# Lightning attention and MLP on one core: pair 5 in chunks of 64 tokens, pair 7 in two parts, v loads behind transposes

## The chip, the core and the metric

The kernel runs on one core of a Trainium2 chip. The metric is the device time in microseconds (us) of one execution; the profile of one execution gives the span from its first to its last instruction and what every engine did in it. The engines are PE (matrix products, results in PSUM), DVE (vector), ACT (scalar activations), POOL (GpSimd) and SP, whose queue issues nearly all DMAs of this kernel in the order in which they stand in it.

## The reference

Inputs q, k, v have the shape (batch 4, heads 8, tokens 768, dim 64). First comes a causal attention with a decay per head, block by block of 64 tokens with a running 64x64 state; then a residual MLP with normalisation. Cut to what matters:

```python
for b in range(nb):                       # nb = 768 / 64
    intra = einsum('bhic,bhjc->bhij', qb, kb) * Dmask        # Dmask: lam^(i-j), causal
    intra = einsum('bhij,bhjd->bhid', intra, vb)
    inter = einsum('bhid,bhde->bhie', qb * lam_pow, kv_state)
    out[:, :, sl] = intra + inter
    kv_state = lam_block * kv_state + einsum('bhsd,bhse->bhde', kb * rev_pow, vb)
x = out.transpose(0, 2, 1, 3).reshape(4, 768, 512)
xn = (x - mean(x)) / sqrt(var(x) + 1e-6) * g_ln
y = x + maximum(xn @ w_ch1, 0) @ w_ch2     # w_ch1 512x2048, w_ch2 2048x512
```

The answer doesn't depend on the block length: with the matching powers of the decay a block may have 128 tokens as well.

## The kernel before

A work unit, called a pair below, is one batch element's 256 tokens: two tiles of 128. There are 12 of them, u = 0 to 11; u % 4 is the batch element, u // 4 the third of the sequence. Each pair goes through the same steps:

- `load_one` or `load_window`: k, q, v from HBM to SBUF (tags kin, qin, vin, three buffers each). Pairs below `LB` are loaded by one DMA of 512 KB for each tensor with runs of 512 bytes (L71), two neighbouring tokens in a row; the others by two DMAs of 256 KB with runs of 256 bytes (L75), one token in a row.
- `p0`: POOL casts k (`in_k`, L199), scales q and casts it (`in_q`, L210) and scales v into vb (`in_v`, L216).
- `transpose_dma`: two DMA transposes on SP make kqT from kq (L231); pairs 0 to 2 use PE instead (L224).
- For a pair below `LB`, in chunks of 128: `kv` (L281, 32 matmuls of 64x64, out to pk), `scores` in two halves (L247, 16 matmuls each with 128 columns), `mask` on DVE (L257, four of 128x512), `new_state` (DVE add L291, POOL decay L287), `av` (L393, 64 matmuls of 64x64), `inter` twice (L406, 16 matmuls each).
- For the others, in chunks of 64: `kv64` (L346, 32), `scores64` (L327, 32 with 64 columns), `mask64` (L333, two of 128x512), `states64` twice (two DVE adds L362 and L365, POOL decay L287 and a cast L370), `av64` (L380, 32), `inter` twice. `keep64` is their mask, made by `make_keep64`.
- `norm`: ACT copies po to x (L428), DVE takes statistics (L430, L431) and writes xc (L435). `to_xT`: a DMA transpose on SP for each tile makes x^T (L451).
- The MLP of the pair (`mlp`): 8 items m1 of 8 matmuls with 128x256 (L484), each followed by ACT's relu (L487), then 8 items m2 of 4 matmuls with 128x512 (L522), four for each tile, after which DVE adds x (`finish`, L543) and SP stores the rows (L550).

Nothing is ordered by a scheduler: `manual_schedule` keeps the order in which the program calls the steps. Pairs 0 and 1 are written out by hand; there L484 stands between their attention steps by `m1s(m1a, chunk, lo, hi)`, which runs a part of the MLP items of pair 0 that use one of the four chunks of w1. All else hangs on one list, `plan`, of MLP items in the order in which PE runs them: n = 0 to 5 finish pair 1's m1, 6 to 21 are m2 of pairs 0 and 1, and from 22 on 16 items belong to each pair from 2 on (pair 3 from 38, pair 4 from 54, pair 5 from 70). `add(n, (step, ...))` puts steps behind item n: each engine and queue gets its instructions at that place of its own order. Pair 6 has its pieces merged with those of pair 5 in two parts, `X1` at n = 56 and `X2` at n = 60; from pair 7 on all is one part, `X`, at n = 73, 89 and so on.

Every DMA of SP signals on one of eight semaphores in turn, and a DMA waits until the one eight places before it has landed. PSUM has four buffers of tag mm, which the MLP's pm and the attention's pk share, two of tag sc and one each of po0 and po1.

Of the kernel before, what the change touches and what calls it, by code (L numbers as in the profile page):

```python
# [16 lines left out]
def kernel(  # L17
# [11 lines left out]
    nc = tc.nc  # L29
# [7 lines left out]
    NP = H // 2  # L37
# [15 lines left out]

    half = [slice(0, 64), slice(64, 128)]
    XB = 3
    LB = 6

    def mm_tile(shape, dtype, name):
        return ps.tile(shape, dtype, tag="mm", bufs=4, name=name)
# [8 lines left out]
    def fill(got, name, u, hs):  # L68
        src = dict(k=k, q=q, v=v)[name]
        if u < LB:  # L70
            nc.sync.dma_start(got[:, hs], source(src, u, hs))  # L71
# [6 lines left out]
    def load_one(u, name):  # L78
        got = inp.tile([128, H, 2 * D], F32, tag=name + "in", name=name + "in")
        fill(got, name, u, slice(0, H))  # L80
        qkv_in.setdefault(u, {})[name] = got.rearrange("p h (j d) -> p h j d", j=2)

    def load_window(u, after_pool=False, parts=1):
        got = {name: inp.tile([128, H, 2 * D], F32, tag=name + "in", name=name + "in") for name in "kqv"}
        if after_pool:

            nc.gpsimd.memset(got["k"][:, 0, 0:1], 0.0)
        n = H // parts
        order = [(name, i) for i in range(parts) for name in "kq"] + [("v", i) for i in range(parts)]
        for name, i in order:  # L90
            hs = slice(i * n, (i + 1) * n)
            fill(got[name], name, u, hs)
        qkv_in[u] = {name: f.rearrange("p h (j d) -> p h j d", j=2) for name, f in got.items()}
# [107 lines left out]
    def in_q(u, eng, hs=ALL):  # L201
        src = qkv_in[u]["q"][:, hs].rearrange("p (a e) j d -> p a e j d", e=2)
        dst = part(1, st[u]["kq"], hs)
        if u < LB:
            lq = lam_q[:, hs, :].rearrange("p (a e) j -> p a e j", e=2)
# [7 lines left out]
    def in_v(u, eng, hs=ALL):  # L213
        n = hs.stop - hs.start
        lv = lam_v[:, hs, :, None] if u < LB else lam_p[:, 1, hs, None, None]
        eng.tensor_tensor(st[u]["vb"][:, hs], qkv_in[u]["v"][:, hs], lv.to_broadcast([128, n, 2, D]), op=ALU.mult)  # L216
# [53 lines left out]
    def kv(u, tag="mm"):  # L270

        s = st[u]
        cc, b = divmod(u, B)
        n_ab = 2 if (cc + 1) * W < S else 1
        bufs = dict(mm=4, sc=2, po=1)[tag]
        pk = [ps.tile([128, 2, NP, D], F32, tag=f"po{ab}" if tag == "po" else tag, bufs=bufs, name=f"pk{ab}")[:, 0] for ab in range(n_ab)]
        for p in range(NP):
            for j in range(2):
                for e in range(2):
                    for ab in range(n_ab):  # L280
                        nc.tensor.matmul(pk[ab][half[e], p, :], lhsT=s["kq"][half[ab], 0, p, j, e],  # L281
                                         rhs=s["vb"][half[ab], 2 * p + e, j],
                                         start=(p == 0 and j == 0), stop=(p == NP - 1 and j == 1), skip_group_check=True)
        s["pk"] = pk
# [46 lines left out]
    def mask64(u, e):  # L331
        s = st[u]
        nc.vector.tensor_tensor(s["mA"][:, e], s["sc"][e],  # L333
                                keep64[:, None, None, :].to_broadcast([128, NP, 2, D]), op=ALU.mult)
# [38 lines left out]
    def av64(u):  # L373
        s = st[u]
        s["po"] = [ps.tile([128, H, D], F32, tag=f"po{ab}", name=f"po{ab}") for ab in range(2)]
        for p in range(NP):
            for e in range(2):
                for j in range(2):
                    for ab in range(2):
                        nc.tensor.matmul(s["po"][ab][half[j], 2 * p + e, :], lhsT=s["mA"][half[ab], e, p, j],  # L380
                                         rhs=s["vb"][half[ab], 2 * p + e, j],
                                         start=(p == 0 and e == 0), stop=False, skip_group_check=True)

    def av(u, pairs, chunks=(0, 1)):
        s = st[u]
        if "po" not in s:
            s["po"] = [ps.tile([128, H, D], F32, tag=f"po{ab}", name=f"po{ab}") for ab in range(2)]
        for p in pairs:
            for e in range(2):
                for j in range(2):  # L390
                    for jq in range(2):
                        for ab in chunks:
                            nc.tensor.matmul(s["po"][ab][half[jq], 2 * p + e, :],  # L393
                                             lhsT=s[f"mA{p // 2}"][half[ab], e, p % 2, j, half[jq]],
                                             rhs=s["vb"][half[ab], 2 * p + e, j],
                                             start=(p == 0 and e == 0 and j == 0), stop=False, skip_group_check=True)
# [22 lines left out]
    def norm(u, ab, early=False):  # L419
        s = st[u]  # L420
        po = s["po"][ab].rearrange("p h d -> p (h d)")
        if "x" not in s:
            s["x"] = xp.tile([128, 2, DM], F32, tag="x", name="x")
            s["mv"] = xp.tile([128, 2, 2], F32, tag="mv", name="mv")
            s["xc"] = wk.tile([128, 2, DM], BF16, tag="xc", name="xc")
        x, mv, xc = s["x"][:, ab], s["mv"][:, ab], s["xc"][:, ab]
        if not early:
            nc.scalar.copy(x, po)  # L428
        stats = wk.tile([128, 6], F32, tag="stats", name="stats")
        nc.vector.bn_stats(stats, po if early else x)  # L430
        nc.vector.bn_aggr(mv, stats)  # L431
        n_h = 2 if u == 0 else 1
        for h in range(n_h):
            sl = slice(h * DM // n_h, (h + 1) * DM // n_h)
            nc.vector.scalar_tensor_tensor(xc[:, sl], in0=po[:, sl], scalar=mv[:, 0:1], in1=g_row[:, sl],  # L435
                                           op0=ALU.subtract, op1=ALU.mult)
# [92 lines left out]
    def rows_of(u):  # L529

        cc, b = divmod(u, B)
        order = "(c p j) d -> j p c d" if u < LB else "(j c p) d -> j p c d"
        return out[b, cc * W:(cc + 1) * W, :].rearrange(order, c=2, j=2)
# [104 lines left out]
    m1a, m2a = mlp(0)  # L638
    m1b, m2b = mlp(1)

    def m1s(f, c, lo=0, hi=2):
        n = f.count // NWC
        for u in range(c * n + lo * n // 2, c * n + hi * n // 2):
            f(u)
# [17 lines left out]
    mask(1, 0)  # L662
    mask(1, 1)
    m1s(m1a, 1, 0, 1)
    kv(1, "sc")
    new_state(1, 0, nc.scalar)
    m1s(m1a, 1, 1, 2)
    rstd_of(0)
    m1s(m1a, 2, 0, 1)
    av(1, (0, 1))  # L670
# [21 lines left out]
    load_w2(3)  # L692
    in_v(2, nc.gpsimd)
    load_window(3, after_pool=True)
    load_window(4)

    def p0(u, k_eng=None):
        open_window(u)
        in_k(u, k_eng or nc.gpsimd)
        in_q(u, nc.gpsimd)  # L700
        in_v(u, nc.gpsimd)

    def s0(u):
        kv(u, "po")
# [15 lines left out]
    def wind_up(u):  # L720


        s = st[u]
        if u < LB:
            av(u, range(NP))
# [71 lines left out]


    def X1(u):
        av(u - 1, range(NP))  # L800
        inter(u - 1, 0)
        kv64(u)
        states64(u, 0)
        states64(u, 1)

    def X2(u):
        scores64(u)
        inter(u - 1, 1)
        mask64(u, 0)
        norm(u - 1, 0)  # L810
        norm(u - 1, 1)
        mask64(u, 1)

    def X(u):

        if u - 1 < LB:
            av(u - 1, range(NP))
# [25 lines left out]
    def add(at, *steps):  # L843
        after.setdefault(at, []).extend(steps)
# [6 lines left out]
    add(8, (s0, 2))  # L851
    add(10, (s3, 2))
    add(12, (s4, 2), (p4, 2), (p0, 3, nc.vector), (transpose_dma, 3))
    for n, name in zip((14, 15, 16), "kqv"):
        add(n, (load_one, 5, name))
    add(15, (rstd_of, 2))
    add(17, (p0, 4))
    add(25, (s1, 3))
    add(25, (transpose_dma, 4))
    add(27, (s2, 3))  # L860
    add(28, (p0, 5))
    add(29, (s3, 3))
    add(30, (s4, 3), (p4, 3))
    for n, name in zip((30, 31, 32), "kqv"):
        add(n, (load_one, 6, name))
    add(34, (rstd_of, 3), (make_keep64,))
    add(37, (transpose_dma, 5))
    add(38, (s1, 4))
    add(39, (p0, 6))
    add(40, (s2, 4))  # L870
    add(42, (s3, 4))
    add(44, (s4, 4), (p4, 4))
    add(46, (transpose_dma, 6))
    add(50, (s1, 5), (rstd_of, 4))
    add(53, (s2, 5))
    for j in range(6, NU):
        at = 55 + 16 * (j - 6)
        if j > 6:
            for n, name in zip((23, 21, 19), "kqv"):
                add(at - n, (load_one, j, name))  # L880
            add(at - 13, (p0, j))
            add(at - 8, (transpose_dma, j))
        if j < LB:
            add(at, (s1_s3, j))
            add(at + 4, (s2_s4, j), (p4, j - 1))
        else:
            if j == 6:
                add(at + 1, (X1, j))
                add(at + 5, (X2, j), (p4, j - 1))
            else:  # L890
                add(at + 2, (X, j), (p4, j - 1))
        add(at + 9, (rstd_of, j - 1))
# [34 lines left out]
```

## Time and profile before

| | |
|---|---|
| median of 10 runs | 216.37 us (214.58 to 218.42) |
| the profiled execution | 217.85 us, its span 216.1 us |
| PE busy, matmuls | 202.8 us (94%), 2884 |
| DVE, ACT, POOL busy | 103.3, 87.3, 79.8 us |
| mean granted PE clock | 0.991 |
| L484 (m1), L522 (m2) | 87.9 us and 81.1 us busy |
| DMA | 37.13 MB, 68385 of 94142 packets under 512 bytes |

Between the span and the execution's time lie 1.75 us of start and end. In a line of the timeline the columns are the start in us from the span's start, the length in us, the engine (PEld is PE's weight load, SPq the DMAs that SP issues), the line of the kernel, the operation, out<-in, the shapes and how many instructions were merged; the bracket is the idle time of the engine before it and what ended it. In a line of the stretches the columns are the stretch, its length, the busy time and the count of PE, PEld, DVE, ACT and POOL, the granted clock of PE, the share of the DMA engines and GB/s.

### The profile page before, as it was taken

The page shows a single profiled execution, that of the slowest core. Times are in us where ns is not written, and L with a number is a line of the kernel's source. Part 1 is how long each engine was busy: PE and PEld are TensorE (multiplying, and loading weights), DVE is VectorE, ACT ScalarE, POOL GpSimd, SP SyncE. Part 2 cuts the span into 40 slices and gives each one's busy share as a digit, 9 for nine tenths or more (in the row PEclk, how much of TensorE's full clock was granted, in tenths as well). Part 3 has the DMA queues.
Part 4 walks back from the last instruction along what each step waited for, and adds up shares of the span by engine and source line. Part 5 has one row for each costly group of instructions (what it writes and reads, how often), then busy time and mean ns, then how long its engine had stood idle before and what let it go on. Part 6 is the DMA issues. An engine that isn't in the chain of part 4 may idle for free.

```text
span 216.1 us, 6642 instructions
## 1 busy us (share of the span) xinstructions
PE 202.8 (94%) x2884; PEld 138.3 (64%) x2899; DVE 103.3 (48%) x225; ACT 87.3 (40%) x165; POOL 79.8 (37%) x111
## 2 busy tenths in 40 slices
PE   2988799999999999999999999999999999999992
PEld 0466579644685575585586585684784874865862
DVE  2688263448256445746438256165184292532011
ACT  3766548511253145055064163271370460641610
POOL 4745339147546073219118229047065020000000
PEclk9999799999999999999999999999999999999999
DMA  4999999999899899699799999998999611320304
GB/s 118 292 272 208 214 255 163 226 298 229 188 317 176 188 211 185 95 221 213 129 217 205 139 227 192 176 201 185 206 210 169 149 25 30 99 52 0 97 2 96
DMA packets 94142, 37.13 MB, mean 172 GB/s; under 512 B 68385, under 2 KB 91169, under 8 KB 94114
## 3 DMA queue, kind: packets, MB, share of 16 engines
q1 hardware_dynamic: 89584, 32.38, 72.3%
q0 software_dynamic: 4224, 4.19, 12.3%
q8 instruction: 22, 0.36, 0.7%
q10 hardware_dynamic: 306, 0.14, 0.3%
q14 instruction: 6, 0.05, 0.1%
HBM read 27.27 MB, written 6.29 MB: 155 GB/s over the span
## 4 chain that ended last, share of the span: by engine, by line
PE 85%; DMA 6%; SPq 3%; DVE 2%; issue 1%; POOL 1%
PE pm L484 37%; PE pm L522 37%; DMA vin<-in_v_dram 6%; SPq L71 3%; PE pm2h L513 2%; PE po L393 1%; PE po L406 1%; PE sc L247 1%; PE po L380 1%; PE pk L281 1%; POOL vb L216 1%; PE sc L327 1%; PE pm1t L496 1%; PE pk L346 1%; DVE xc L435 1%
## 5 line engine op out<-in xcount | busy, mean ns | idle before, releaser
L487 ACT ACTIVATE hT<-pm 128x512 bf16<-128x512 f32 x92 | 55.0, 601 | 90.9 <-PE pm L484 90.8
L484 PE MATMUL pm<-xT,w 128*128 128x256 bf16 x736 | 87.9, 276 | 1.0 <-DMA w<-in_moe_w_ch_dram 0.8
L522 PE MATMUL pm<-w,hT 128*128 128x512 bf16 x353 | 81.1, 379 | 1.0 <-issue 0.3
L484 PEld LDWEIGHTS <-w 128*128 128x128 bf16 x736 | 70.7, 99 | 13.4 <-DMA w<-in_moe_w_ch_dram 1.0
L522 PEld LDWEIGHTS <-hT 128*128 128x128 bf16 x368 | 35.5, 98 | 40.0
L543 DVE SCALAR_TENSOR_TENSOR o<-pm,rstd,x 128x512 f32<-128x512 f32 x23 | 17.1, 748 | 43.4 <-PE pm L522 43.3
L287 POOL TENSOR_TENSOR Sn<-Stmp,lam_s 128x256 bf16<-128x256 f32 x16 | 9.8, 614 | 73.7 <-DVE Stmp L365 49.6
L435 DVE SCALAR_TENSOR_TENSOR xc<-po,mv,g_row 128x512 bf16<-128x512 f32 (+1 forms) x24 | 16.8, 705 | 1.8
L257 DVE TENSOR_TENSOR mA<-sc,keep 128x512 bf16<-128x512 f32 x20 | 13.1, 684 | 6.8 <-PE sc L247 6.8
L428 ACT COPY x<-po 128x512 f32<-128x512 f32 x18 | 9.9, 588 | 11.3 <-PE po L393 5.3
L430 DVE BATCH_NORM_STATS2 stats<-x 128x6 f32<-128x512 f32 x18 | 12.4, 687 | 4.0 <-ACT x L428 3.9
L417 DVE COPY seen<-po 128x8 f32<-128x8 f32 x18 | 2.3, 162 | 23.8 <-PE po L406 23.8
L216 POOL TENSOR_TENSOR vb<-vin,lam_v 128x1024 bf16<-128x1024 f32 (+1 forms) x7 | 11.6, 1658 | 4.4 <-DMA vin<-in_v_dram 3.4
L210 POOL TENSOR_TENSOR kq<-qin,lam_p 128x512 bf16<-128x512 f32 x12 | 12.3, 1044 | 0.7 <-DMA qin<-in_q_dram 0.7
L210 POOL TENSOR_TENSOR kq<-qin,lam_q 128x512 bf16<-128x512 f32 x10 | 10.6, 1084 | 3.8 <-DMA qin<-in_q_dram 3.8
L216 POOL TENSOR_TENSOR vb<-vin,lam_p 128x1024 bf16<-128x1024 f32 x6 | 11.4, 1898 | 1.0 <-DMA vin<-in_v_dram 0.9
L199 POOL CAST kq<-kin 128x512 bf16<-128x512 f32 (+1 forms) x18 | 10.5, 613 | 1.6 <-DMA kin<-in_k_dram 1.6
L333 DVE TENSOR_TENSOR mA<-sc,keep 128x512 bf16<-128x512 f32 x12 | 8.2, 682 | 1.4 <-PE sc L327 1.4
L406 PE MATMUL po<-Sn,kqT 64*64 64x64 bf16 x216 | 7.5, 199 | 0.0
L224 PE MATMUL tp<-ident,kq 128*128 128x128 bf16 x48 | 6.0, 262 | 0.5 <-ACT kq L199 0.2
L406 PEld LDWEIGHTS <-kqT 64*64 64x64 bf16 x304 | 5.3, 108 | 1.5 <-issue 1.5
L224 PEld LDWEIGHTS <-kq 128*128 128x128 bf16 x48 | 3.7, 112 | 3.9 <-DVE kq L199 1.5
(98 smaller groups left out, 145.9 us busy)
## 6 DMA issues: line engine op xcount, KB each, us to landing
out_dram<-o SPq DMA_DIRECT2D x22, 256.0 KB, 4.6
w<-in_moe_w_ch_dram POOLq DMA_DIRECT2D x8, 512.0 KB, 9.2
kin<-in_k_dram SPq DMA_DIRECT2D x14, 256.0 KB, 3.6
qin<-in_q_dram SPq DMA_DIRECT2D x14, 256.0 KB, 5.0
vin<-in_v_dram SPq DMA_DIRECT2D x14, 256.0 KB, 5.9
kin<-in_k_dram SPq DMA_DIRECT2D x5, 512.0 KB, 6.2
qin<-in_q_dram SPq DMA_DIRECT2D x5, 512.0 KB, 7.6
vin<-in_v_dram SPq DMA_DIRECT2D x5, 512.0 KB, 8.4
```

Of the source, the lines that this page charges most:

```text
L199: (eng.copy if eng is nc.scalar else eng.tensor_copy)(dst[:, :, :, j], src[:, :, :, j])
L210: eng.tensor_tensor(dst[:, :, :, j], src[:, :, :, j], lq[:, :, :, j:j + 1].to_broadcast([128, n, 2, D]), op=ALU.mult)
L216: eng.tensor_tensor(st[u]["vb"][:, hs], qkv_in[u]["v"][:, hs], lv.to_broadcast([128, n, 2, D]), op=ALU.mult)
L257: nc.vector.tensor_tensor(s[f"mA{hf}"][:, e], s[f"sc{hf}"][e], kp[:, None, :, :].to_broadcast([128, 2, 2, 128]), op=ALU.mult)
L406: nc.tensor.matmul(s["po"][ab][half[jq], 2 * p + e, :], lhsT=qT[half[e], p, jq, half[ab]], rhs=s["S"][ab][jq][half[e], p, :], start=False, ...
L428: nc.scalar.copy(x, po)
L430: nc.vector.bn_stats(stats, po if early else x)
L435: nc.vector.scalar_tensor_tensor(xc[:, sl], in0=po[:, sl], scalar=mv[:, 0:1], in1=g_row[:, sl], op0=ALU.subtract, op1=ALU.mult)
L484: nc.tensor.matmul(pm[:, b, :], lhsT=w1[n // W2K][:, kk, (n % W2K) * 128:(n % W2K + 1) * 128], rhs=xT_of[g][:, kk, 0:N], start=(b == 0 and ...
L487: nc.scalar.activation(hT[:, u * NB:(u + 1) * NB, 0:N], pm, ACT.Relu)
L522: nc.tensor.matmul(acc[i], lhsT=hT[:, kk, i * 128:(i + 1) * 128], rhs=w2[kk // W2K][:, kk % W2K, :], start=(kk == 0), stop=(kk == KB - 1))
L543: nc.vector.scalar_tensor_tensor(o[:, ab], in0=a, scalar=rstd[:, ab:ab + 1], in1=x[:, ab], op0=ALU.mult, op1=ALU.add)
```

## The change

Pair 5 is now in the group with chunks of 64 (`LB` 6 to 5): a new step `A(5)` at n = 51 does its kv64, scores64, masks and states in one piece, and `X1` and `X2` use `av64`. Pair 7 also goes by `X1` and `X2`, at n = 72 and 76. In the hand-written part a stretch of pair 0's MLP stands ahead of pair 1's `kv` rather than behind it. The v loads of pairs 4, 5 and 6 are issued later on SP, each behind the x^T transposes of an earlier pair (2, 3 and 4), and `in_v` of these pairs is taken out of `p0` and stands later on POOL. The steps of pair 4 stand two or three items later, and its k/q transposes behind the x^T transposes of pair 3.

```diff
-    LB = 6
+    LB = 5
...
     m1s(m1a, 1, 0, 1)
+    m1s(m1a, 1, 1, 2)
     kv(1, "sc")
     new_state(1, 0, nc.scalar)
-    m1s(m1a, 1, 1, 2)
...
-    load_window(4)
+    load_one(4, "k")
+    load_one(4, "q")
...
     def p0(u, k_eng=None):
...
-        in_v(u, nc.gpsimd)
+        if u not in (4, 5, 6):
+            in_v(u, nc.gpsimd)
...
     def X1(u):
-        av(u - 1, range(NP))
+        av64(u - 1)
...
+    def A(u):
+        kv64(u)
+        scores64(u)
+        states64(u, 0)
+        mask64(u, 0)
+        states64(u, 1)
+        mask64(u, 1)
...
-    for n, name in zip((14, 15, 16), "kqv"):
+    for n, name in zip((18, 19, 31), "kqv"):
         add(n, (load_one, 5, name))
-    add(17, (p0, 4))
+    add(17, (load_one, 4, "v"), (p0, 4))
     add(25, (s1, 3))
-    add(25, (transpose_dma, 4))
     add(27, (s2, 3))
-    add(28, (p0, 5))
+    add(31, (p0, 5))
     add(29, (s3, 3))
-    add(30, (s4, 3), (p4, 3))
-    for n, name in zip((30, 31, 32), "kqv"):
+    add(30, (s4, 3), (p4, 3), (transpose_dma, 4))
+    for n, name in zip((32, 33), "kq"):
         add(n, (load_one, 6, name))
+    for n, u in ((26, 4), (43, 5), (52, 6)):
+        add(n, (in_v, u, nc.gpsimd))
     add(37, (transpose_dma, 5))
-    add(38, (s1, 4))
-    add(39, (p0, 6))
-    add(40, (s2, 4))
-    add(42, (s3, 4))
-    add(44, (s4, 4), (p4, 4))
-    add(46, (transpose_dma, 6))
-    add(50, (s1, 5), (rstd_of, 4))
-    add(53, (s2, 5))
+    add(41, (s1, 4))
+    add(42, (p0, 6))
+    add(43, (s2, 4))
+    add(44, (s3, 4))
+    add(46, (s4, 4), (p4, 4))
+    add(46, (load_one, 6, "v"), (transpose_dma, 6))
+    add(51, (A, 5), (rstd_of, 4))
...
-            if j == 6:
+            if j in (6, 7):
                 add(at + 1, (X1, j))
                 add(at + 5, (X2, j), (p4, j - 1))
```

## The prediction

> **What bounds the kernel now.** I read the page's busy rows first, then its slices, then the stretches of the matrix engine's clock, then the timeline around the two places that the diff touches.
>
> ```profile
> PE 202.8 (94%) x2884; PEld 138.3 (64%) x2899; DVE 103.3 (48%) x225; ACT 87.3 (40%) x165; POOL 79.8 (37%) x111
> PE   2988799999999999999999999999999999999992
> PEclk9999799999999999999999999999999999999999
> ```
>
> PE is busy all the time but in slices 0 to 4 (5.4 us each), so after 27 us only PE work removed or a new PE wait can move the end. The one dip of the clock is in slice 4. Busy time by stretches of 3.41 us around it:
>
> ```profile
> 20.99:24.41 3.42, 1.48 (x41) 1.19 (x42) 1.84 (x4) 1.70 (x3) 2.12 (x3) 1.00 1.24 206
> 24.41:27.82 3.41, 3.41 (x19) 2.18 (x16) 0.17 (x1) 1.71 (x6) 0.00 (x0) 0.50 1.14 243
> ```
>
> The first column after the stretch's length is PE busy, the third from the end the granted clock. PE is busy for 1.48 of 3.42 us, and in the next stretch it has half its clock: 3.41 x 0.5 = 1.7 us lost. The timeline shows what it waited for:
>
> ```profile
> 21.33 1.05 PE L484 MATMUL pm<-xT,w 128*128 128x256 bf16 x8 [0.81 <-DMA w<-in_moe_w_ch_dram]
> 22.03 1.90 POOL L216 TENSOR_TENSOR vb<-vin,lam_v 128x1024 bf16<-128x1024 f32 x1 [2.60 <-DMA vin<-in_v_dram]
> 23.98 0.45 PE L281 MATMUL pk<-vb,kq 64*64 64x64 bf16 x32 [1.60 <-POOL vb L216]
> 24.36 1.02 PE L484 MATMUL pm<-xT,w 128*128 128x256 bf16 x4
> ```
>
> PE stands for 1.60 us until POOL has scaled pair 1's v, which landed at 22.0. The second place is the end of pair 4 (norm, transposes) and pair 5's pieces:
>
> ```profile
> 81.89 0.32 PE L406 MATMUL po<-Sn,kqT 64*64 64x64 bf16 x16
> 84.88 2.86 SPq L451 DMA_TRANSPOSE xT<-xc  x2
> 85.77 0.75 DVE L435 SCALAR_TENSOR_TENSOR xc<-po,mv,g_row 128x512 bf16<-128x512 f32 x1
> 87.43 0.45 PE L281 MATMUL pk<-vb,kq 64*64 64x64 bf16 x32
> 88.26 2.54 PE L522 MATMUL pm<-w,hT 128*128 128x512 bf16 x11 [0.16 <-issue]
> 90.73 0.42 PE L247 MATMUL sc<-kqT 64*64 64x128 bf16 x16
> 93.80 0.71 PE L393 MATMUL po<-vb,mA 64*64 64x64 bf16 x64
> 94.46 0.48 PE L346 MATMUL pk<-vb,kq 64*64 64x64 bf16 x32
> ```
>
> Here PE runs without a wait; what matters is the distance from pair 4's last piece (over at 82.14) to pair 6's kv (94.46), and that the transposes of pair 4 leave SP only at 87.74.
>
> **What the Trainium skill says.** "TensorE: Matmul & The Clock Gate", Part 1 (the HAM clock gate): the clock is halved after a window of about 3.4 us with too little matmul work, the windows run freely, and it comes back after a busy one. The trace agrees (3.41 us at 0.50). It does not show the threshold: 1.48 of 3.42 us busy was too little, 2.76 of 3.41 in the stretch before was enough. "DMA: Bandwidth & Descriptors", Specifications: transfers under 512 B are below line rate. Pair 5's loads go from 512 B runs to 256 B runs; the page's DMA issues have 512 KB of k in 6.2 us, and each of two 256 KB halves in 3.6, issued 0.6 apart, so the trace shows no penalty that a single load would feel.
>
> **The change part by part.** The profiled execution took 217.85 us (span 216.1), 1.5 above the median of 216.37, about one half-clock stretch; I make the sum on it and carry the difference to the median.
>
> (1) Eight pair-0 matmuls (L484, the second half of w1 chunk 1) go ahead of pair 1's kv. Their weights are there: the first half ran at 21.33 from the same chunk. They fill 1.05 us of the 1.60 us wait; kv still starts at 23.98, and everything behind is **1.05 us** earlier. In that stretch PE would be busy 2.5 of 3.4 us, so I expect the full clock to be kept: **1.7 us** more, if it was lost in a given execution. What is late next: pair 2's q (scaled by POOL 32.47 to 34.88, PE's transposes at 37.27) leaves 2.4 us, pair 3's k/q transposes 2 us.
>
> (2) Pair 4's v load goes from ahead of pair 2's x^T transposes to behind them and behind pair 3's k/q. SP spent 3.5 us (46.38 to 49.89) on it, so these transposes can leave up to 3.5 us earlier. PE had no wait for them (pair 2's MLP began at 56.76 with no gap), so the gain is 0 by itself; it keeps (1) from ending in a wait at x^T. Pair 4's v is scaled at n = 26 and used at 41: 15 items, some 14 us. Moving pair 4's k/q transposes behind pair 3's x^T costs 0: scores of pair 4 come three MLP items (2.8 us) later too.
>
> (3) Pair 5 with chunks of 64. Before: kv with half the scores 87.43 to 88.26 (0.83, a 0.16 gap in it), other half 90.73 to 91.08 (0.35), av and first inter 93.80 to 94.46 (0.66): 1.84 us. After, at the rows of pair 7: kv and scores 0.60 (111.20 to 111.76 and an entry), av64 and inter 0.45 (110.75 to 111.20): 1.05. **Saved 0.8 us** on PE. DVE loses two masks of 0.68 and gets two adds of 0.43, POOL two copies of 0.40; DVE is 48% and POOL 37% busy, and the PSUM slots that they free are wanted over 0.9 us later: 0. Pair 5's k, q, v become six DMAs of 256 KB, spread over a longer stretch: 0.
>
> (4) Pair 7's merged piece in two parts. Pair 6 had that form: 93.80 to 94.87 and 98.47 to 98.98, 1.58 less 0.21 for its longer av, 1.37; the one-part form took 1.28 (110.75 to 112.03). **Cost 0.1 us.** x^T of pair 6 then leaves 4.4 us after the second part, as pair 5's did, and is wanted some 7.7 us after it: 0.
>
> (5) The v loads of pairs 5 and 6 go behind transposes. For pair 5 SP runs x^T(3), k/q(4), then v5, k6, q6; POOL scales k6, q6, then v5. Six such DMAs land within 10 us elsewhere, so v5 is scaled about 0.8 us before pair 5's kv: 0. **For pair 6 it doesn't fit.** v6 is issued behind x^T(4), which waits for DVE's xc of pair 4. Count from the end of pair 4's last inter. PE's way to pair 6's kv: 20 matmuls of L522 4.4, pair 5's piece 0.6, 8 of L522 1.7, 24 of L484 2.7, av64 and inter 0.45: 9.85 us. v6's way: xc done at 4.4 (86.52 - 82.14; some 0.2 less, ACT being free sooner), second transpose issued by 5.4, both halves of v6 issued from there, landed 4.5 later (3.6 for one and the second's later start), POOL's scaling 1.90, a hand-over of 0.1: 11.9. **PE waits 2.1 us** for vb, where before it waited for nothing. The waiting instruction heads PE's queue, so the rest of the MLP of pairs 4 and 5 stands behind it, and k/q(6) transposes behind v6 on SP have time. Bounds: 1.2 if both halves land in 3.6, 4.1 if in 6.5 (the page's 5.9 for v, and 0.6). I take 2.1 because nothing but x^T(4) is in flight then.
>
> (6) A wait of 2.1 us can halve the clock for a window by itself: all of it lies in one window in (3.41 - 2.1)/3.41 = 40% of phases, most of it in more; and 64x64 matmuls stand around it. I put 55% on it, price 1.7 us.
>
> Sum: -1.05 - 0.8 + 0.1 + 2.1 = **+0.35 us**, and half-clock windows: one lost at 24 us, one got after the wait. On the profiled execution 218.2, on the median 216.7.
>
> **The rivals.** About 0.5% (1.1 us) is what a measurement of this kernel can tell from no change.
>
> A, likeliest (0.36): gains and the new wait cancel, and a half-clock window takes the place of the other: 216.6.
>
> B (0.28): as A, but the wait straddles windows in most executions and the clock stays full: 216.7 - 1.7 = 215.0. For it: the free-running windows. Against: the 43% busy stretch that did trip.
>
> C, slower (0.30): v6 comes at the crowded price. Place: pair 6's kv behind POOL's vb; price 4.1 instead of 2.1 and the half-clock window with certainty: 216.7 + 2.0 = 218.7. It decides from a wait of 2.9 us on (216.7 + 0.8 is 217.5, half a per cent above). For it: v loads took 5.9 in the median, DMA is over 90% busy till 170 us. Against: SP is empty before these two.
>
> D, faster (0.06): the load does not do what I say, since SP reaches v6 earlier or PE comes later than counted, and the wait is under 0.5: 216.7 - 1.6 - 1.7 = 213.4.
>
> **How the numbers follow.** Faster by over 0.5%: B and D, 0.34. Within: A, 0.36. Slower: C, 0.30. The time is A's, 216.6. From 214.7 (B) to 218.5 (near C's end) leaves out D and the tail of C. A's own range is 215.4 to 217.5.
>
> **What the changed profile would show.** (1) PE's wait for vb before kv at 24 us down to about 0.55, no 0.50 stretch there. (3) no L247 of pair 5, L380 instead of L393. (5) "PE pk <- POOL vb" with about 2.1 us near 92, POOL waiting for the landing of vin; if instead PE waits for x^T(4) or for nothing, the main step is wrong. (6) a half-clock stretch just after. If the first waits are unchanged, or a long wait stands elsewhere (pair 4's or 5's kv), the accounts of (1) or (2) fail.

## Result and the profile after

The changed kernel takes **217.59 us** (median of 14 runs, 216.47 to 218.48) against 216.18 us for the kernel before in the same comparison (51 runs, 214.03 to 218.61). The ratio is **1.0087, 95% interval 1.006 to 1.0114**: slower by somewhat under 1%. It compares the fast runs alone, those within 1.5% of the quickest of their kernel, and so isn't the quotient of the two medians (1.0065), here and below. The range of the forecast, 214.7 to 218.5, holds it; the likeliest case, within 0.5%, does not: the kernel is on the slower side, between case A (216.6) and case C (218.7).

The profiled execution of the changed kernel took 218.52 us, its span 216.8; that is longer than each of the 14 timed runs and 0.93 above their median. The page's busy row and slices:

```profile
PE 201.5 (93%) x2852; PEld 137.9 (64%) x2867; DVE 104.1 (48%) x225; ACT 87.4 (40%) x165; POOL 80.6 (37%) x113
...
PE   2988999999999899679999999999999999999993
...
PEclk9999999999999999999999999999999999999999
```

32 matmuls are gone, the dip of slice 4 is gone from both rows, and a new dip (6 and 7 tenths) stands in slices 16 and 17, counted from 0, which are 86.7 to 97.6 us. The clock is full throughout. PE's timeline shows both places; a line that has no bracket began with no wait to speak of:

```profile
21.45 1.92 PE L484 MATMUL pm<-xT,w 128*128 128x256 bf16 x16 [0.71 <-DMA w<-in_moe_w_ch_dram]
23.60 0.45 PE L281 MATMUL pk<-vb,kq 64*64 64x64 bf16 x32 [0.23 <-POOL vb L216]
...
70.85 3.65 PE L484 MATMUL pm<-xT,w 128*128 128x256 bf16 x32 [0.31 <-DMA xT<-xc]
...
75.55 0.42 PE L247 MATMUL sc<-kqT 64*64 64x128 bf16 x16 [0.67 <-DMA kqT<-kq]
...
86.51 0.45 PE L346 MATMUL pk<-vb,kq 64*64 64x64 bf16 x32
...
87.14 0.45 PE L327 MATMUL sc<-kqT 64*64 64x64 bf16 x32 [0.18 <-DMA kqT<-kq]
...
87.74 1.67 PE L522 MATMUL pm<-w,hT 128*128 128x512 bf16 x7 [0.16 <-issue]
...
90.72 2.78 PE L484 MATMUL pm<-xT,w 128*128 128x256 bf16 x24 [1.30 <-DMA xT<-xc]
...
95.52 0.44 PE L346 MATMUL pk<-vb,kq 64*64 64x64 bf16 x32 [1.51 <-POOL vb L216]
```

Pair 0's matmuls now run through (x16), and pair 1's kv waits 0.23 instead of 1.60. Then five new waits stand between 70 and 96 us. The other bracket, [0.16 <-issue], stands in the profile of before too (88.26). An account of the two profiled executions, in three stretches:

| stretch | before | after | after is later by |
|---|---|---|---|
| start of pair 3's MLP | 73.25 us | 70.85 us | -2.40 (1.7 of it the half clock at 24 us) |
| from there to pair 6's kv | 21.21 | 24.67 | +3.46 |
| from there to the end of the span | 121.64 | 121.28 | -0.36 |

The middle stretch in both profiles (the number behind the length is PE's busy time):

```profile
73.25:94.46 21.21, 20.96 (x423) 14.47 (x427) 12.29 (x24) 7.69 (x14) 7.51 (x9) 1.00 0.93 177
70.85:95.52 24.67, 20.79 (x391) 14.21 (x393) 11.73 (x26) 7.94 (x14) 10.20 (x12) 1.00 1.14 184
```

PE's idle time there went from 0.25 us to 3.88, of which 3.82 is in the brackets above (0.67 + 0.18 + 0.16 + 1.30 + 1.51); its own work went from 20.96 to 20.79 us. Leaving the half clock aside, the change brought 0.70 us ahead of pair 3, lost 3.46 behind it and got 0.36 back: 2.4 us more than that execution of before, its half clock taken off. This is an account of one execution of each kernel; the medians are 1.41 apart.

What PE waited for, on SP's and POOL's timelines (SP's lengths are those of the issuing instructions, not of the transfers):

```profile
85.19 2.52 SPq L451 DMA_TRANSPOSE xT<-xc  x2
87.77 2.38 SPq L75 DMA_DIRECT2D vin<-in_v_dram  x2
```

```profile
93.57 1.90 POOL L216 TENSOR_TENSOR vb<-vin,lam_p 128x1024 bf16<-128x1024 f32 x1 [2.96 <-DMA vin<-in_v_dram]
```

This is the chain of the prediction: x^T(4), v6 right behind it, POOL idle until vin lands, the scaling, pair 6's kv. But x^T(4) is late too, and that is new: its transposes leave SP at 87.71, which before was 87.74. In the kernel before PE came to them at 91.08:

```profile
91.08 2.79 PE L484 MATMUL pm<-xT,w 128*128 128x256 bf16 x24
```

After, it came at 89.42 (87.74 + 1.67 and an entry). PE got there 1.66 us earlier; x^T(4) did not, and its second transpose landed at 90.58, 4.08 us after its issue began. The two waits are not two separate losses: v6's landing and POOL's scaling set pair 6's kv at 95.52 whatever PE does ahead of it, so without the wait of 1.30 PE would have stood 2.81 for vb.

### The profile page after: what moved, and what is told of

It reads as the page before. It is cut to its first block, busy times and chain, and to the rows that moved or that the text cites. A ratio compares the mean times of both kernels' runs of the same rounds, so it can differ in the third digit from the quotient of the medians.

```text
span 216.8 us, 6587 instructions
## 1 busy us (share of the span) xinstructions
PE 201.5 (93%) x2852; PEld 137.9 (64%) x2867; DVE 104.1 (48%) x225; ACT 87.4 (40%) x165; POOL 80.6 (37%) x113
## 2 busy tenths in 40 slices
DMA packets 97262, 37.13 MB, mean 171 GB/s; under 512 B 74577, under 2 KB 94289, under 8 KB 97234
## 4 chain that ended last, share of the span: by engine, by line
PE 72%; DMA 13%; SPq 7%; POOL 3%; DVE 2%; issue 1%; POOLq 0%
PE pm L522 33%; PE pm L484 30%; DMA vin<-in_v_dram 8%; SPq L71 4%; SPq L75 3%; DMA qin<-in_q_dram 2%; DMA kqT<-kq 2%; POOL vb L216 2%; PE pm2h L513 2%; PE po L406 1%; PE pk L346 1%; PE po L380 1%; PE po L393 1%; POOL kq L210 1%; PE sc L327 1%
## 5 line engine op out<-in xcount | busy, mean ns | idle before, releaser
L484 PE MATMUL pm<-xT,w 128*128 128x256 bf16 x736 | 85.9, 273 | 2.3 <-DMA xT<-xc 1.6
L522 PE MATMUL pm<-w,hT 128*128 128x512 bf16 x353 | 81.3, 379 | 1.0 <-issue 0.3
L484 PEld LDWEIGHTS <-w 128*128 128x128 bf16 x736 | 70.1, 98 | 14.2 <-issue 1.8
L522 PEld LDWEIGHTS <-hT 128*128 128x128 bf16 x368 | 35.3, 98 | 39.8
L543 DVE SCALAR_TENSOR_TENSOR o<-pm,rstd,x 128x512 f32<-128x512 f32 x23 | 17.1, 745 | 37.4 <-PE pm L522 37.4
L216 POOL TENSOR_TENSOR vb<-vin,lam_p 128x1024 bf16<-128x1024 f32 x7 | 13.3, 1898 | 6.9 <-DMA vin<-in_v_dram 6.9
L210 POOL TENSOR_TENSOR kq<-qin,lam_p 128x512 bf16<-128x512 f32 x14 | 14.4, 1044 | 1.3 <-DMA qin<-in_q_dram 1.2
L257 DVE TENSOR_TENSOR mA<-sc,keep 128x512 bf16<-128x512 f32 x16 | 10.5, 686 | 7.5 <-PE sc L247 7.5
L216 POOL TENSOR_TENSOR vb<-vin,lam_v 128x1024 bf16<-128x1024 f32 (+1 forms) x6 | 9.8, 1647 | 6.2 <-DMA vin<-in_v_dram 6.2
L333 DVE TENSOR_TENSOR mA<-sc,keep 128x512 bf16<-128x512 f32 x14 | 9.6, 682 | 2.8 <-PE sc L327 2.8
L210 POOL TENSOR_TENSOR kq<-qin,lam_q 128x512 bf16<-128x512 f32 x8 | 8.2, 1045 | 7.0 <-DMA qin<-in_q_dram 7.0
L362 DVE TENSOR_TENSOR Smid<-pk,Sn 128x256 f32<-128x256 f32 x14 | 5.9, 425 | 4.2 <-PE pk L346 1.6
L461 ACT ACTIVATE std<-mv,eps_t 128x2 f32<-128x2 f32 x12 | 3.6, 298 | 8.0 <-DVE mv L431 8.0
```

Source lines behind the costliest of these rows:

```text
L210: eng.tensor_tensor(dst[:, :, :, j], src[:, :, :, j], lq[:, :, :, j:j + 1].to_broadcast([128, n, 2, D]), op=ALU.mult)
L257: nc.vector.tensor_tensor(s[f"mA{hf}"][:, e], s[f"sc{hf}"][e], kp[:, None, :, :].to_broadcast([128, 2, 2, 128]), op=ALU.mult)
L484: nc.tensor.matmul(pm[:, b, :], lhsT=w1[n // W2K][:, kk, (n % W2K) * 128:(n % W2K + 1) * 128], rhs=xT_of[g][:, kk, 0:N], start=(b == 0 and ...
L522: nc.tensor.matmul(acc[i], lhsT=hT[:, kk, i * 128:(i + 1) * 128], rhs=w2[kk // W2K][:, kk % W2K, :], start=(kk == 0), stop=(kk == KB - 1))
L543: nc.vector.scalar_tensor_tensor(o[:, ab], in0=a, scalar=rstd[:, ab:ab + 1], in1=x[:, ab], op0=ALU.mult, op1=ALU.add)
```

## The experiments

The theory of the prediction is that of **v6**: the new wait for it behind x^T(4) is what costs, and the rest is small. The rivals: **the queue**, in which SP has no slack between 40 and 100 us, so that loads and transposes costed at nothing move it, and what PE saves ends in waits for transposes; **the clock**, in which half-clock windows decide; and **the form**, in which the time is in pair 5's chunks of 64. Each expectation names the theories it tells apart in its own words.

### Part 1 alone, and the change without it

```diff
 before_m1s (from the kernel before; after_no_m1s undoes the same in the changed kernel)
     m1s(m1a, 1, 0, 1)
+    m1s(m1a, 1, 1, 2)
     kv(1, "sc")
     new_state(1, 0, nc.scalar)
-    m1s(m1a, 1, 1, 2)
```

> The kernel before with part (1) of the change alone: eight matmuls of pair 0 go ahead of pair 1's kv. Order theory (the later waits of the changed kernel come from where v and the transposes stand on SP, so they don't exist here): PE's wait before kv falls from 1.60 to about 0.3 to 0.55 us, no half-clock stretch, and the end is 1.05 to 1.5 us earlier than before (2.7 in an execution that had the half-clock stretch). Supply theory (what DMA and SP can deliver by 50 to 95 us is fixed in absolute time): the gain is given back as waits for x^T or k/q transposes between 54 and 95 us, and the time is within 0.5 us of before.

> The changed kernel with part (1) undone. Order theory: the waits near 90 to 95 us are counted from the end of pair 4's last inter, so they stay at 2.8 us in sum and the kernel is 1.05 us or more slower than the changed one (218.6 or more). Supply theory: PE comes later to the same deadlines, the waits of 4.1 us between 70 and 96 us shrink by what is lost at 24 us, and the time stays within 0.5 us of the changed kernel's 217.6.

Part 1 alone: 216.23 against 215.81 us, ratio 1.001 (0.9984 to 1.0036). Its profiled execution was one of its quickest (214.71), with PE running into pair 1's kv without a wait:

```profile
22.27 0.45 PE L281 MATMUL pk<-vb,kq 64*64 64x64 bf16 x32
```

But that is no gain of part 1: in most profiled executions of the old order pair 1's kv does not wait either. before_x7, whose order is that of before up to there, has

```profile
19.84 1.92 POOL L216 TENSOR_TENSOR vb<-vin,lam_v 128x1024 bf16<-128x1024 f32 x1
21.82 0.60 PE L281 MATMUL pk<-vb,kq 64*64 64x64 bf16 x32
```

POOL begins to scale pair 1's v at 19.2 to 20.6 us in 10 of the 14 profiled executions and at 21.7 to 22.0 in four: those of before, after, after_no_m1s and before_pair4_late. Of the six that run pair 1's kv at its old place and without idle work, before and after_no_m1s wait 1.60 and 1.61 us, and before_x7, before_lb5, before_load5_256 and before_v4_late not at all. Part 1 fills a wait that most of these executions don't have, which goes with a median that gains nothing. What makes v land late in some is open.

The change without part 1: 218.21, ratio 1.0103 (1.0059 to 1.0148), 0.16% above the changed kernel by the ratios and 0.6 us by the medians, so between the two expectations. Its waits (in all in us, how often, the longest):

```profile
PE pk L281 <- POOL vb L216: 1.8, 2, 1.6
PE pk L346 <- POOL vb L216: 1.5, 1, 1.5
PE pm L484 <- DMA xT<-xc: 1.4, 1, 1.4
```

The first is back, the last two are as in the changed kernel. They do not shrink when PE comes later through the first 25 us, so it looks as if they hang on a chain that moves with PE's order: pair 4's pieces, norm, x^T(4), v6.

### Filling the first wait with idle work

```diff
 before_fill
     m1s(m1a, 1, 0, 1)
+    keep_busy(5, "po0")     # 5 matmuls of 128x512
     kv(1, "sc")
```

> The kernel before with five extra matmuls of 128x512 (about 1.1 us of PE, result never read) in PE's wait before pair 1's kv. If the half clock comes from too little matmul work in that window, the 0.50 stretch at 24 to 28 us is gone and an execution that had it ends 1.7 us earlier; the wait itself stays filled and gives nothing, so in the median -0.3 to -1.2 us. If the dip has another cause, it stays and the time is the same as before.

216.85 against 215.81, ratio 1.0043 (1.0016 to 1.0071). Keeping PE busy there gains nothing, and there is hardly anything to save: of 135 runs of the kernel before that stand beside the experiments three had a mean clock of 0.991 or 0.992 (one more, of 298.43 us, had 0.677; single runs of before_m1s and before_fill, 238.22 and 241.12 us, had 0.86), and one window of 3.41 us at half clock takes 1.7 of 216 us, or 0.008, off the mean. The stretch at 0.50 in the prediction's profile was that of a rare execution. In the profile of before_fill POOL began to scale pair 1's v at 19.27, so there was no wait to fill: the idle matmuls put kv at 23.18, where the four executions above have it at 21.8 to 22.1. Whether such work would keep the clock where v is late was not seen.

### X(7) in two parts alone

```diff
 before_x7 (X1 takes av64 where pair u - 1 has chunks of 64)
-            if j == 6:
+            if j in (6, 7):
```

> The kernel before with pair 7's merged piece alone in two parts. Prediction's view: 0.1 us of PE, the time within 0.3 us of before. Rival: x^T(6) comes too late for its MLP, 1 us or more.

216.27 against 216.22, ratio 0.9995 (0.9964 to 1.0027): nothing, as predicted. This profile is worth more as a look at the kernel before without the late v and the half clock, since up to 90 us its order is the same. PE's timeline:

```profile
55.14 3.65 PE L484 MATMUL pm<-xT,w 128*128 128x256 bf16 x32 [0.77 <-DMA xT<-xc]
...
72.29 1.03 PE L484 MATMUL pm<-xT,w 128*128 128x256 bf16 x8 [0.55 <-DMA xT<-xc]
```

There are waits for x^T(2) and x^T(3) that the profile of before did not have (before_fill has them too, 0.68 and 0.53). In that profile x^T(2) landed at 55.72, and PE came later:

```profile
56.76 3.66 PE L484 MATMUL pm<-xT,w 128*128 128x256 bf16 x32
```

In before_x7 PE came at 54.37 (55.14 - 0.77), 2.4 us earlier. The late v and the half clock of that one execution hid that PE would otherwise have stood.

### v4's load alone

```diff
 before_v4_late
-    load_window(4)
+    load_one(4, "k")
+    load_one(4, "q")
...
-    add(17, (p0, 4))
+    add(17, (load_one, 4, "v"), (p0, 4))
+    add(26, (in_v, 4, nc.gpsimd))
```

> The kernel before with pair 4's v load alone moved behind x^T(2) and pair 3's k/q transposes, its scaling to n = 26. Prediction's view: 0 within 0.5 us (ratio 0.998 to 1.002), no wait at x^T(2), which lands 1.5 us or more earlier. Rival: the load now stands ahead of pair 4's k/q transposes and pair 3's x^T and puts these back by up to 2 us: a wait at x^T(3) near 73 us and a ratio of 1.004 to 1.008.

219.03 against 216.22, ratio 1.0136 (1.0062 to 1.021; 6 runs, from 216.99 to 221.64). PE's timeline, from a quick execution (217.09):

```profile
71.86 1.03 PE L484 MATMUL pm<-xT,w 128*128 128x256 bf16 x8 [1.35 <-DMA xT<-xc]
```

x^T(2) left SP at 50.67 instead of 53.53 and no longer holds PE; the load that was taken from ahead of it now stands ahead of x^T(3), which does. The wait has moved from 55 to 72 us and grown. The "0 by itself" of the prediction is refuted, though three of the six runs have a mean clock of 0.984 to 0.992, so that a part of the loss is half clock; the two at 1.0 took 216.99 and 217.09.

### The two halves of pair 5's change: its loads, and its chunks

```diff
 before_load5_256 (in load_window's and load_one's common part)
+        if u == 5:
+            for j in range(2):
+                nc.sync.dma_start(got[:, hs, j * D:(j + 1) * D],
+                                  source(src, u, hs)[:, :, j * D:(j + 1) * D])
+            return
 before_lb5 (A is that of the changed kernel, X1 takes av64; all loads at their old places)
-    LB = 6
+    LB = 5
...
-    add(50, (s1, 5), (rstd_of, 4))
-    add(53, (s2, 5))
+    add(50, (A, 5), (rstd_of, 4))
```

> The kernel before with pair 5's k, q and v each loaded by two DMAs with runs of 256 bytes instead of one with 512, same data in the same places. Prediction's view: no cost, 0 within 0.3 us. Supply theory: 3072 more packets put SP and the DMA engines back by some 2 us around 56 to 66 us, pair 4's and pair 3's transposes come later and PE waits: 1 us or more slower.

> The kernel before with pair 5 in chunks of 64 alone (LB 5, its pieces as one step at n = 50), all loads and transposes in their old places. Prediction's view: 0.8 us less PE work, so 0.4 to 0.8 us faster than before. Supply theory: pair 5's loads in runs of 256 bytes cost what they cost in the kernel that only split them (ratio to before 1.0135), and the saving on PE is small against it: ratio 1.009 to 1.014, with a wait of 2 us or more for pair 3's x^T near 73 us.

The loads alone, same bytes in runs of 256 instead of 512 bytes and in six DMAs instead of three: 218.67 against 215.81, ratio **1.0135** (1.0094 to 1.0177). The whole form alone, LB = 5: 217.99 against 215.97, ratio 1.0072 (1.0041 to 1.0103). PE's timeline of the former, where every line number is 5 higher (L489 is L484), and two stretches from the wait on:

```profile
73.17 1.03 PE L489 MATMUL pm<-xT,w 128*128 128x256 bf16 x8 [2.53 <-DMA xT<-xc]
```

```profile
70.90:74.31 3.41, 1.14 (x28) 0.89 (x32) 0.53 (x1) 0.01 (x1) 0.00 (x0) 1.00 0.59 128
74.31:77.72 3.41, 3.41 (x61) 2.50 (x50) 2.14 (x4) 1.18 (x2) 1.95 (x4) 0.50 1.22 234
```

The wait for x^T(3) is 2.53 us, PE is busy for 1.14 of 3.41 us, and a window at half clock follows. 4 of its 6 runs have a mean clock of 0.992 or less, and 12 of 22 of LB = 5, so in these orders the half clock is a usual part of the loss, which it is not in the changed kernel (none of 15). It is not all of it: the two full-clock runs of the loads alone took 217.77 and 218.74, and the ten of LB = 5 have a median of 217.0. LB = 5 waits for x^T twice, 2.17 us until 56.00 and 1.89 until 74.81, in a profile that is one of its slower ones (219.42).

In both, PE waits for x^T(3) about 2 us where before_x7 waits 0.55: the form of pair 5 costs through the queue. SP spends 6.5 us on issuing the six DMAs of pair 5 in before_load5_256, where before spends 2.2 on the three. Which of the two it is, the short runs or the number of DMAs, the experiment does not part. The 2.17 at x^T(2) cannot come from pair 5's loads, which stand behind x^T(2) in the queue. How little PE itself gains by the form is read further down.

### Pair 4's steps later

```diff
 before_pair4_late (and part 1)
-    add(25, (transpose_dma, 4))
...
-    add(30, (s4, 3), (p4, 3))
+    add(30, (s4, 3), (p4, 3), (transpose_dma, 4))
-    add(38, (s1, 4))
+    add(41, (s1, 4))
...
-    add(44, (s4, 4), (p4, 4))
+    add(46, (s4, 4), (p4, 4))
```

> The kernel before with part (1), with pair 4's k/q transposes behind pair 3's x^T, and with pair 4's steps at the changed kernel's places; pair 5 stays in chunks of 128 with runs of 512 bytes and the v loads stay where they were. Supply theory: pair 3's x^T leaves SP 1 us or more sooner, nothing was added to the DMA queue, so the gain of part (1) is kept: 1.0 to 1.5 us faster than before (ratio 0.993 to 0.995). Order theory of pair 4 (its k/q transposes are now late for its scores): a wait of 0.5 to 1 us at pair 4's scores, and the time is that of before.

217.23 against 215.97, ratio 1.0073 (1.0043 to 1.0103). Neither expectation had a loss. Its profiled execution (219.02) is among its slowest and has the late v of pair 1, so PE comes to x^T(2) no earlier than in before_x7 (54.39 against 54.37); x^T(2) leaves SP 0.6 us later, and PE waits 1.41 us for it instead of 0.77. x^T(3) no longer holds PE, and x^T(4) now does, as in the changed kernel. PE's timeline:

```profile
55.80 2.45 PE L484 MATMUL pm<-xT,w 128*128 128x256 bf16 x21 [1.41 <-DMA xT<-xc]
...
91.89 2.79 PE L484 MATMUL pm<-xT,w 128*128 128x256 bf16 x24 [0.73 <-DMA xT<-xc]
```

### The changed kernel without v6, or without pair 5's loads

```diff
 after_no_v6 (pair 6 takes pair 5's v)
-    add(46, (load_one, 6, "v"), (transpose_dma, 6))
+    add(46, (lambda: qkv_in[6].update(v=qkv_in[5]["v"]),), (transpose_dma, 6))
 after_no_load5 (pair 5 takes pair 4's k, q and v)
-        add(n, (load_one, 5, name))
+        add(n, (lambda name=name: qkv_in.setdefault(5, {}).update({name: qkv_in[4][name]}),))
```

> The changed kernel without the load of pair 6's v; pair 6 reads pair 5's v in its place (this leaves part of the input out). Order theory: the wait of 1.5 us before pair 6's kv goes, and the one for pair 4's x^T (1.3 us) too, as far as it came from v6's packets behind it on the same engines: 1.5 to 2.8 us less, 215 to 216. Supply theory: the x^T wait stays at 1.3 and some 0.5 us is gained.

> The changed kernel without pair 5's loads of k, q and v; pair 5 reads pair 4's in their place (this leaves part of the input out). Supply theory: with six DMAs of 256 KB fewer between 57 and 76 us the waits at pair 3's x^T (0.3) and at pair 4's and pair 5's scores (0.7, 0.2) go, those at 90 to 96 us shrink: 1 to 2.5 us less. Order theory: those at 90 to 96 us stay at 2.8, and the kernel is 0.5 to 1.2 us faster than the changed one.

Without v6: 215.87 against 215.97, ratio **1.0008** (0.9976 to 1.004). Its waits for vb are gone; those for x^T(4) and kqT(4) stay:

```profile
PE pm L484 <- DMA xT<-xc: 1.2, 1, 1.2
PE sc L247 <- DMA kqT<-kq: 0.8, 1, 0.8
```

Without pair 5's bytes: 217.73 against 215.97, ratio 1.0079 (1.0049 to 1.0109), no better than the changed kernel, and its last waits are even longer:

```profile
PE pm L484 <- DMA xT<-xc: 1.8, 1, 1.8
PE pk L346 <- POOL vb L216: 1.7, 1, 1.7
```

In the changed order, then, pair 5's small runs aren't what costs; taking out the one load of v6 takes the kernel back to the time of before, while taking out three loads of pair 5 does not, as the theory of v6 has it. This shows what the load costs where it stands, not that another place is better. That x^T(4) is late without v6 too shows that its wait has another cause.

### v6 earlier

```diff
 after_v6_early
-    for n, name in zip((32, 33), "kq"):
+    for n, name in zip((32, 33, 34), "kqv"):
...
-    add(46, (load_one, 6, "v"), (transpose_dma, 6))
+    add(46, (transpose_dma, 6))
```

> The changed kernel with pair 6's v load back beside its k and q (n = 34, ahead of pair 5's k/q transposes on SP) and nothing else undone. If the place of v6 behind x^T(4) is by itself the loss: the wait before pair 6's kv goes, and the time falls by 1.3 to 1.7 us to that of the kernel without this load (215.9). If SP's queue between 70 and 90 us is full, so that v6 only changes place with what stands behind it: v6's two issues (2.4 us) put pair 5's k/q transposes and x^T(4) back, PE waits 2 us more at pair 5's scores or at x^T(4), and the time stays within 0.6 us of the changed kernel's 217.6.

Five of its six runs lie between 220.8 and 221.8 us, at a mean clock of 0.982 to 0.989, one at 215.97 at full clock, which is the time that the repair was to bring; with such a split there is no ratio. PE's timeline of a run of the five:

```profile
86.95 0.45 PE L346 MATMUL pk<-vb,kq 64*64 64x64 bf16 x32 [0.67 <-POOL vb L216]
...
91.25 0.52 PE L327 MATMUL sc<-kqT 64*64 64x64 bf16 x32 [3.86 <-DMA kqT<-kq]
```

v6 in front delays k/q(5)'s transposes, PE stands 3.86 us for them, and a window at half clock follows. The obvious repair of the wait is in most executions worse than the wait: the theory of v6 has the place right, and that of the queue fits why moving the load does not cure it.

### Both orders together, pair 5 as before

```diff
 both_parts_lb6: before_pair4_late and before_v4_late together, and
-    for n, name in zip((14, 15, 16), "kqv"):
+    for n, name in zip((18, 19, 20), "kqv"):
```

> The changed kernel with pair 5 back in chunks of 128 (LB 6, 512-byte runs), the v loads of pairs 5 and 6 beside their k and q, and pair 7 in one part; what stays is part (1), pair 4's v behind x^T(2), and pair 4's steps and transposes late. Against the kernel that had all of this but the place of v4 (ratio 1.0073, a wait of 1.4 us at x^T(2)): that wait goes. If the place of v4 is what keeps the gain of part (1): ratio to before 0.993 to 0.998. If the late steps of pair 4 cost by themselves (x^T(4) comes 2 us later for an MLP that doesn't move): the wait of 0.7 to 1.3 us at x^T(4) stays and the ratio is 1.000 to 1.004.

216.29 against 216.22 in medians, ratio 1.004 (1.0014 to 1.0067), as the second of the two expectations had it. This has part 1, v4 behind x^T(2) and pair 4 late, but v5 and v6 beside their k and q and chunks of 128 for pair 5. The waits for x^T(2) and x^T(3) are gone, and what is left of such waits is at pair 4:

```profile
PE pm L484 <- DMA xT<-xc: 0.6, 1, 0.6
PE sc L247 <- DMA kqT<-kq: 0.4, 1, 0.4
```

It is the best of the orders that move loads, and no better than the kernel before. No version tried beats the kernel before.

### What the runs say together

When the second transpose of x^T(2) and of x^T(3) leaves SP in each profiled execution, and PE's waits for them:

| kernel | x^T(2) out | x^T(3) out | between | wait x^T(2) | wait x^T(3) |
|---|---|---|---|---|---|
| before (half clock at 24 us) | 53.53 | 71.91 | 18.4 | 0 | 0 |
| before_fill | 52.87 | 71.14 | 18.3 | 0.68 | 0.53 |
| before_x7 | 52.88 | 70.96 | 18.1 | 0.77 | 0.55 |
| before_m1s | 51.53 | 68.64 | 17.1 | 0.16 | 0 |
| before_load5_256 | 51.53 | 71.82 | 20.3 | 0 | 2.53 |
| before_lb5 | 53.73 | 73.45 | 19.7 | 2.17 | 1.89 |
| before_v4_late | 50.67 | 70.47 | 19.8 | 0 | 1.35 |
| before_pair4_late | 53.48 | 70.41 | 16.9 | 1.41 | 0 |
| both_parts_lb6 | 50.95 | 68.23 | 17.3 | 0 | 0 |
| after | 51.05 | 69.43 | 18.4 | 0 | 0.31 |

This is the theory of the queue: where pair 4's k/q transposes stand ahead of x^T(3), SP issues without a gap from x^T(2) to x^T(3), and what is put into that stretch (v4, pair 5's loads in six DMAs) comes out as a wait of PE. Where they are taken out (before_pair4_late, both_parts_lb6) SP stands idle for 4.4 and 2.5 us until DVE has written xc, x^T(3) leaves on DVE's time, and PE does not wait. The table scatters too: before_m1s, with the order of before on SP, has 17.1 where the first three have 18.1 to 18.4. The changed kernel fits this: v4 behind x^T(2) frees that, k/q(4) behind x^T(3) makes the room for v4 and for pair 5's loads. What it frees at 55 and 72 us it gives back at 76, 90 and 95.

## Why the prediction was right or wrong, step by step

**(1) m1s moved, -1.05 and the half clock: right for its profile, wrong for the median.** The wait fell from 1.60 to 0.23, no half clock stood there, and the two profiled executions show -1.01 (0.70 and the 0.31 lost again at x^T(3)). But the median gained nothing (1.001): the wait was in two of six executions with the old order, and a clock of 0.991 or 0.992 in 3 of 135 runs of the kernel before. The prediction took one execution's late v for the kernel's. The bookkeeping should have caught the half clock: the prediction itself put the profiled execution one half-clock stretch above the median, so the median could not hold that stretch, and cases B and D took 1.7 us off a time that did not have it.

**(2) v4 behind x^T(2) and pair 4's transposes and steps later, 0: this is the step that failed.** It rested on "pair 2's MLP began with no gap", read in an execution that was 2.4 us late at that point. In before_x7 and before_fill x^T(2) and x^T(3) hold PE for 0.7 and 0.5 us. v4 moved alone costs 1.36%. And the later steps of pair 4 are not free: s4 goes from item 44 to 46, so that PE has 8 matmuls of L484 and 4 of L522 less between pair 4's last piece and pair 4's MLP: 7.33 us (82.09 to 89.42) instead of 8.94 (82.14 to 91.08), while norm and issue take as long as ever. PE so came early for x^T(4), and 1.30 us became a wait because the landing took 4.08 us; with the 2.4 of other executions x^T(4) would have landed at 88.9, ahead of PE. The prediction named a wait for x^T(4) as what would make its main step wrong, and did not work it out: its own 4.4, 0.6 and 1.7 bring PE there at 6.7, and a transpose that is out by 5.4 and was begun 1.2 earlier lands at 7.8 with the 3.6 us that the page of before has as the median. As the wait for vb follows, this one cost the changed kernel nothing of its own; without v6 it is what stays (1.2). The move of the k/q transposes cost 0.67 at kqT(4) and 0.31 at x^T(3).

**(3) Pair 5 in chunks of 64, -0.8 on PE and 0 for the loads: wrong in both.** PE's work in the stretch is 20.96 before and 20.79 after, 0.17 less. The rows of pair 7, from which 1.05 us was taken, are of pieces packed one behind the other; between waits kv64 and scores64 cost 0.89 (86.51 to 87.74, less the waits of 0.18 and 0.16) instead of 0.60, and scores of pair 4 that ran overlapped with kv before (74.48 behind 74.21) now stand alone. The loads "spread over a longer stretch: 0" cost 1.35% by themselves at their old places; "no penalty that a single load would feel" looks at the load, and the loss is in what stands behind it. In the changed order they cost nothing that after_no_load5 could show.

**(4) X(7) in two parts, +0.1: right**, 0.9995 (0.9964 to 1.0027).

**(5) v6 behind x^T(4), a wait of 2.1 for vb: the mechanism was right, the size short.** PE does wait for vb at pair 6's kv, POOL does wait for vin, and without the load the loss is gone. From the end of pair 4's last inter (82.09): x^T(4) was issued by 5.6 (5.4 predicted), v6 landed at 11.3, 5.7 after its issue began (4.5 predicted: the term that was mis-sized), and kv ran at 13.4 (11.9 predicted). PE's own way without waits was 10.3 (9.85 predicted). So PE lost 3.15 us where 2.1 was said, 1.51 of it at vb and 1.30 already at x^T(4), and v6's chain alone sets the sum. v5 in time: right, no wait for vb at pair 5.

**(6) A half-clock window in 55%: it didn't come.** 15 of 15 runs are at 0.998 or more. The loss came in two waits of 1.30 and 1.51 us with 3.3 us of work between them, not in one of 2.1; the windows of the trace keep 1.95 us of work or more (see the last section).

**The sum.** At full clock +0.35 was predicted, and the two profiled executions differ by 2.4:

| term | predicted | profiled executions |
|---|---|---|
| (1) | -1.05 | -1.01 |
| (2): x^T(3) 0.31, kqT(4) 0.67 | 0 | +0.98 |
| (3) on PE | -0.8 | -0.17 |
| (4), and what came back behind pair 6 | +0.1 | -0.36 |
| (5): 1.51, 1.30 and 0.18, less 0.03 of small gaps | +2.1 | +2.96 |

The medians differ by less, 1.41. That goes with the waits at x^T(2) and x^T(3) in the usual execution of the kernel before (0.77 and 0.55 in before_x7), which its profile did not show and of which the change removes most, and with a profile of the changed kernel that is 0.93 above its median; no run parts the two. **Luck.** The range of 3.8 us held a time that the sum missed by 2 us in the profiles. The forecast of 218.2 for the profiled execution is near 218.52 because two misses cancel: no new half-clock window (1.7 less) and 2.05 us more of waits and work. **The cases.** C's place and mechanism (pair 6's kv behind vb, at a higher price than A's) are what happened, with a loss of 3.15 rather than 4.1 and without its half clock.

## What to carry to other kernels

A DMA that is moved within a queue without gaps should not be costed at 0: write down what stands behind it at the old place and the new one, and when PE wants each, also where the profile shows no wait. Before a "no wait here" is used, ask how late the consumer was in that very execution; a rare stall upstream hides the waits that bound the usual one. And where steps are moved later in one engine's order, count the work that is left between the producer of a transfer and its user, since that is all the cover the transfer has. Where two waits follow one another, ask whether the second chain alone would set the end of both.

## What was unexpected of the hardware

- **Runs of 256 bytes on a shared queue.** The page of before_load5_256 counts 97262 packets against 94142, 3% more for the same 37.13 MB, and 2.9 us more time. SP's stretch from x^T(2) to x^T(3) took 20.3 us instead of 17.1 to 18.4. "DMA: Bandwidth & Descriptors", Why small descriptors are slow (HBM only), has a fixed overhead for each packet; the runs agree in direction, but the edit also made six DMAs of three. The cost was paid by the transposes behind the loads, and by the half clock that their wait set off.
- **What trips the clock.** The length of a wait does not decide. In before_lb5 a wait of 1.89 us was followed by a window at 0.50 and the one of 2.17 was not. Counting back in steps of 3.41 us from the half-clock window, the 2.17 falls on two windows and the 1.89 lies in one:

```profile
52.08:55.49 3.41, 1.69 (x8) 0.58 (x6) 0.75 (x1) 0.00 (x0) 3.41 (x5) 1.00 1.27 233
72.56:75.97 3.41, 1.52 (x34) 0.92 (x36) 0.75 (x1) 0.04 (x1) 0.00 (x0) 1.00 0.66 142
```

  With all 14 traces cut into windows this way, from about 20 to 200 us, the four that were followed by half clock held 0.23, 1.14, 1.48 and 1.52 us of PE's work (after_v6_early, before_load5_256, before, before_lb5), and none that held 1.69 or more was (1.73 in after_no_load5, 1.95 in the changed kernel). "TensorE: Matmul & The Clock Gate", Why this matters for your kernels, asks for no gap of over some 3 us; here a gap of less than 2 was enough where it fell into one window. Its Part 1 has the windows run freely, which fits: the same two waits, 0.81 and 1.60 us in before and 0.77 and 1.61 in after_no_m1s, tripped in one and not in the other.
- **The landing of a transpose.** The second transpose of x^T(4) landed 4.1 us after its issue began in the changed kernel (86.50 to 90.58), and 3.9 to 4.5 in seven other profiles, after_no_v6, after_no_load5 and before_m1s among them; in before_load5_256, before_fill and before_v4_late it took 2.4, in after_v6_early 2.8. What makes the difference was not settled: the slow landing is there without v6 behind it and without pair 5's loads.
- **Open as well:** why x^T(2) leaves SP at 51.5 us in some executions and at 53 to 53.7 in others of kernels that have the same order up to there. That the spread of the kernel before (214.0 to 218.6) comes from this or from the landing of pair 1's v is argued from the profiles and wasn't shown in timed runs. Nor is it known why the two k/q transposes of pair 4 hold SP for 5.9 us in before and for 2.6 where they stand behind x^T(3).
